# Moving shares and the Q projection in the attention schedule of a fused layernorm, attention and token-MLP kernel

## The chip, the cores and the metric

One core of one Trainium2 chip. The metric is the device time of one execution in microseconds, the median of several runs. The time before is 650.8 us (median of 3 runs, 650.64 to 651.08).

## What is computed

The output is the input, plus a segmented attention with a memory, plus an MLP over the token axis. Cut to what matters here (B = 1, S = 2048 tokens, D = 1024, 32 heads of 32, 4 segments of 512 tokens, F = 3584):

```python
x  = A_x; xn = layernorm(x)
q, k, v = heads(xn @ wq), heads(xn @ wk), heads(xn @ wv)      # 32 heads, 4 segments
for s in range(4):
    p     = softmax(q[s] @ k[s].T * scale + causal_mask)
    a_dot = p @ v[s]
    a_mem = phi(q[s]) @ M / (phi(q[s]) @ z + 1e-6)            # phi(t) = t+1 if t>0 else exp(t)
    o[s]  = g * a_mem + (1 - g) * a_dot
    M += phi(k[s]).T @ v[s];  z += phi(k[s]).sum(tokens)
A = o @ wo
B = (w2.T @ gelu(w1.T @ layernorm(xn) + b1) + b2)             # over the token axis
return x + A + B
```

## The kernel before

**Stages.** First the layernorm and the MLP, up to about 373 us of the profile, as dense products on TensorE; the MLP's result with the residual goes to the output tensor in DRAM as `part`. Then the attention, which is the only stage that the change touches.

**Units.** `attention` runs 32 units, one for each segment (8 units each) and group of four heads. Unit u does:

- *logits* of unit u in up to three steps, here written L(u,0), L(u,1), L(u,2). L(u,0) is key block 0, L(u,1) key blocks 1 and 3, and L(u,2), only in even units, is key block 2 of unit u and of unit u+1. Each step is 4 or 8 small matmuls into PSUM banks 0 to 3, one exponential on ScalarE over the four banks (line 1370), and one or two causal selects on POOL (line 1374).
- *weighing* of unit u-1 in three parts, W0, W1, W2: matmuls into bank 4, 5 and 4 again, each evicted by VectorE (line 1424). In segments 0 to 2, W2 also makes the update of the memory M, with two more VectorE operations (lines 1435, 1437).
- *dense jobs*, of 8 matmuls of 512 columns each: `v_job` (a chunk of V for later units, written here v m.c), `q_job(u + 2)`, `k_job(u + 2)` (up to unit 13), and `wo_job(c, half)` (an output projection of an earlier segment, written wo c.half). Dense jobs use banks 6 and 7 in turn. A job's first matmul waits until the job two before it has been read out of its bank. Who reads it out: ScalarE for q (line 1253) and for v from unit 8 on (line 1299); VectorE for k (save two), for earlier v, and for wo, an addition of `part` (line 1313).
- *side work* of VectorE, a queue `self.side`: `scales`, `products`, `add` (combining the weighed parts of unit u-1; lines 1467 to 1479), `phi_q(u)` (lines 1228, 1230), `phi_k`, and in twelve units one chunk of normalized x for a later segment ("xn": a VectorE scaling, line 1130, and a DMA transpose from SP's queue).

**What sets the order.** All of it is written out in program order, and each engine has its own in-order stream. `cut(total, shares)` turns a tuple of shares into numbers of dense matmuls: those ahead of L(u,0), then ahead of W0, of W1, of W2, of L(u,1), of L(u,2), and the rest. `dense(n)` issues n matmuls of the first jobs; when it has passed a *stop* (a count inside a job: 1, 3, 5, 7 on ScalarE's jobs and 1, 3, 5 on VectorE's in the later units), it issues one piece of side work behind the matmuls. When a job's eighth matmul has been issued, its read-out is issued at once.

A finished q (of unit 8 on) also needs its exponential `etmp` for phi; `late_exps` issues it behind the exponential of the next logits step:

```python
        fw.op("act", lambda e: e.activation(dst, src, ACT.Exp, scale=SCALE), ...)    # logits
        ...
        self.late_exps()                                                              # its last line

            if b is None:                                                             # dense
                b = job[1] = 6 + self.turn
                self.turn ^= 1
```

From unit 18 on, `unit_jobs` fills a quota (24 matmuls in even units, 20 in odd ones) with wo jobs. Where the quota ends inside a job, `self.left` carries its rest (4 matmuls) into the next unit. Before the change, the jobs of a unit stand in the order v, q, wo:

| unit | jobs in order (matmuls left of a carried one in brackets) | carried out |
|---|---|---|
| 18 | v5.2, q20, wo4.0 | |
| 19 | v5.3, q21, wo4.1 | 4 of wo4.1 |
| 20 | wo4.1 [4], v6.0, q22, wo5.0 | 4 of wo5.0 |
| 21 | wo5.0 [4], v6.1, q23 | |
| 22 to 25 | as 18 to 21, with v6.2 ... v7.1, q24 ... q27 | |
| 26, 27 | as 18, 19, with v7.2, v7.3, q28, q29 | 4 of wo7.1 |
| 28 | wo7.1 [4], q30, wo8.0, wo8.1 | 4 of wo8.1 |
| 29 | wo8.1 [4], q31, wo9.0 | |
| 30 | wo9.1, wo10.0, wo10.1 | |
| 31 | wo11.0, wo11.1 | |

In the units from 28 on, all waiting side work is issued ahead of W0. After unit 31 `tail` weighs unit 31 and makes the last four output projections.

Of the kernel before, what the change touches and what calls it, by code (L numbers as in the profile page):

```python
# [30 lines left out]
N_UNIT = N_SEG * N_GRP  # L31
# [355 lines left out]
class _Kernel:  # L387
# [1119 lines left out]
    def unit_jobs(self, u):  # L1507
        jobs = [self.wo_job(*self.wo_jobs.popleft())] if 10 <= u < self.QUOTA_FROM else []
        m = u // 4 + 1
        if m < 2 * N_SEG:  # L1510
            jobs.insert(0, self.v_job(m, u % 4))
        if u + 2 < N_UNIT:
            jobs.append(self.q_job(u + 2))
            if u + 2 < N_UNIT // 2:
                jobs.append(self.k_job(u + 2))
            else:
                self.k_load(u + 2)
        if u >= self.QUOTA_FROM:
            quota = self.QUOTA[u % 2] if u + 1 < N_UNIT else 100
            quota -= 8 * len(jobs) + sum(8 - j[0] for j in self.jobs)  # L1520
            while quota > 0 and self.wo_jobs:
                jobs.append(self.wo_job(*self.wo_jobs.popleft()))
                quota -= 8
            self.left = max(-quota, 0)
        return jobs
# [5 lines left out]
    def attention(self):  # L1531
        self.jobs, self.turn, self.left = deque(), 0, 0
        self.side, self.stops = deque(), self.STOPS
        self.exps, self.in_etmp = [], [None] * 4
        self.wo_jobs = deque((c, half) for c in range(4 * (N_SEG - 1)) for half in range(2))
        self.jobs.extend([self.q_job(0), self.k_job(0)] + [self.v_job(0, c) for c in range(4)])
        self.dense(16)
        self.late_exps()
        self.phi_k(0)
        self.k_transpose(0)  # L1540
        self.jobs.extend([self.q_job(1), self.k_job(1)])
        self.dense(100)
        for u in range(N_UNIT):
            if u == N_GRP:
                t, R = _Walk(self.mem, self.B_AT + self.STG_AT, self.B_AT + self.S2_AT).take(
                    "oT2", [P, N_GRP, SEG_L], BF16, N_GRP)
                self.oT.append(t)
                self.R_oT.append(R)
                self.load_fin(0)
                self.load_fin(1)  # L1550
            if 1 <= u <= N_GRP:
                self.fw.dma(self.wo[:, u - 1, :], self.A_wo[(u - 1) * P:u * P, :], writes=[self.R_wo[u - 1]])
            even = u % 2 == 0
            self.jobs.extend(self.unit_jobs(u))
            total = 8 * len(self.jobs) - sum(j[0] for j in self.jobs) - self.left
            xn = self.XN_AT.index(u) + 4 if u in self.XN_AT else None
            if u in self.XN_AT[::4]:
                self.xn_load(xn)
                self.xn_load(xn + 1)
            if u >= 18 and even:  # L1560
                cuts = self.cut(total, (0, 5, 1, 4, 0, 9, 5))
            elif u >= 18:
                cuts = self.cut(total, (4, 1, 2, 1, 0, 12))
            elif u < 10 or u >= 14 and total <= 26:
                cuts = self.cut(total, (0, 4, 2, 4, 1, 13, 8) if even else (7, 3, 2, 4, 1, 15))
            else:
                cuts = self.cut(total, (0, 4, 2, 2, 2, 14, 8) if even else (7, 3, 2, 2, 2, 16))
            end = u >= N_UNIT - 4
            self.stops = self.STOPS_FEW if total <= 26 and u >= 14 else self.STOPS
            self.dense(cuts[0])  # L1570
            self.logits(u, 0)
            self.dense(cuts[1], end)
            while end and self.side:
                self.side.popleft()()
            if u:
                self.weigh(u - 1, 0)
            self.dense(cuts[2], False)
            if u:
                self.weigh(u - 1, 1)
            self.dense(cuts[3], False)  # L1580
            if u:
                self.weigh(u - 1, 2)
                steps = self.combine(u - 1)
                last = steps[-1]
                steps[-1] = lambda u=u, last=last: (last(), self.o_transpose_dma(u - 1))
                self.side.append(steps.pop(0))
            if N_GRP <= u:
                self.side.append(lambda u=u: self.phi_q(u))
            if u:
                self.side.extend(steps)  # L1590
            if u + 1 < N_UNIT:
                self.side.append(lambda u=u: (self.phi_k(u + 1), self.k_transpose(u + 1)))
            if xn is not None:
                self.side.append(lambda c=xn: (self.xn_scale(c), self.xn_transpose(c), c % 4 < 2 and self.xn_load(c + 2)))
            self.dense(cuts[4])
            self.logits(u, 1)
            if even:
                self.dense(cuts[5])
                self.logits(u, 2)
            self.dense(8 * len(self.jobs) - sum(j[0] for j in self.jobs) - self.left)  # L1600
        while self.side:
            self.side.popleft()()
        self.tail()
# [84 lines left out]
```

## Time and profile before

| | |
|---|---|
| median of 3 runs | 650.8 us |
| profiled execution, time | 650.74 us |
| profiled execution, span from first to last instruction | 649.0 us |
| TensorE (PE) matmul busy | 644.7 us, 99% |
| VectorE (DVE) busy | 435.4 us, 67% |
| ScalarE (ACT) busy | 282.8 us, 44% |
| GpSimd (POOL) busy | 153.9 us, 24% |
| first L(0,0) to first L(31,1) | 387.44 to 628.68 us |

Times inside the profile are from the span's start. Matmul ends are modelled, and a matmul of 512 columns is shown as 380 ns long though the next one starts 216 ns later; so a busy PE may still be waiting, and waits are read from the starts: from the start of one step to the start of the next, less what the step takes elsewhere. ScalarE's and VectorE's shares are means over the whole span; in the attention ScalarE is busy 70 to 90% of the time.

### The profile page before, as it was taken

The numbers are of one execution on the slowest core, as the hardware profiler recorded it, in microseconds if no ns is written. First come the engines' busy times: TensorE is split into PE (matmuls) and PEld (weight loads), VectorE is DVE, ScalarE is ACT, GpSimd is POOL, SyncE is SP. The second block draws the span as 40 slices with busy tenths as digits, with TensorE's granted clock in tenths as the row PEclk, the third lists the DMA queues.
The fourth block names the chain that finished last, engine by engine and source line by source line (L and its number), as shares of the span: only waits on it lengthen the run. The fifth ranks groups of instructions, "written<-read, shape, count | busy, mean of one in ns | idle before, by whom it ended". The sixth has DMA issues, their size and how long they took to land.

```text
span 649.0 us, 11186 instructions
## 1 busy us (share of the span) xinstructions
PE 644.7 (99%) x4611; PEld 304.2 (47%) x4611; DVE 435.4 (67%) x813; ACT 282.8 (44%) x307; POOL 153.9 (24%) x179
## 2 busy tenths in 40 slices
PE   9999999999999999999999999999999999999998
PEld 3444444444444444444444444444455455545544
DVE  6975676665556664744647325766887888887886
ACT  6543232232210000110101037778777878889860
POOL 2500000000001220220202203344334444554450
PEclk9999999999999999999999999999999999999999
DMA  9804233233489947538272947999854675445334
GB/s 303 217 0 131 66 100 96 65 108 87 125 249 205 239 123 211 143 116 227 68 224 84 270 120 179 177 175 225 140 136 102 160 166 122 126 105 130 100 97 139
DMA packets 190123, 95.00 MB, mean 146 GB/s; under 512 B 108664, under 2 KB 176248, under 8 KB 190072
## 3 DMA queue, kind: packets, MB, share of 16 engines
q1 hardware_dynamic: 189928, 94.25, 57.6%
q8 instruction: 36, 0.59, 0.4%
q14 instruction: 15, 0.12, 0.1%
q10 hardware_dynamic: 144, 0.03, 0.0%
HBM read 69.23 MB, written 11.53 MB: 124 GB/s over the span
## 4 chain that ended last, share of the span: by engine, by line
PE 96%; ACT 2%; DVE 1%; DMA 0%; POOL 0%; issue 0%; DVEq 0%
PE ps_all L199 96%; ACT pT L1370 2%; DVE ln_st L587 1%; DMA xin<-in_A_x_dram 0%; DVE h L627 0%; POOL ln_rs L611 0%; ACT qT L1253 0%; ACT vA L1299 0%; DVE ln_mv L590 0%; DVE ln_mv L609 0%; DVE fin L1634 0%; PE ps_all L205 0%; DVEq L70 0%
## 5 line engine op out<-in xcount | busy, mean ns | idle before, releaser
L1370 ACT ACTIVATE pT<-ps_all 128x2048 bf16<-128x2048 f32 x80 | 150.1, 1877 | 41.2 <-PE ps_all L199 41.0
L1374 POOL TENSOR_SCALAR_AFFINE_SELECT pT<-pT 128x512 bf16<-128x512 bf16 x128 | 105.3, 841 | 159.2 <-ACT pT L1370 159.2
L689 DVE TENSOR_TENSOR part<-ps_all,part 128x512 f32<-128x512 f32 x84 | 57.7, 690 | 108.5 <-PE ps_all L199 87.5
L1075 POOL TENSOR_TENSOR part<-part,stg 128x512 f32<-128x512 f32 x24 | 33.0, 1402 | 284.8 <-DVE part L689 284.8
L746 ACT ACTIVATE g<-part,b1c 128x512 f16<-128x512 f32 x36 | 26.0, 722 | 98.7 <-DVE part L689 98.7
L199 PE MATMUL ps_all<-wv,xnT 128*128 128x512 bf16 x256 | 68.7, 380 | 0.3 <-ACT qT L1253 0.2
L199 PE MATMUL ps_all<-xnT,wq 128*128 128x512 bf16 x256 | 65.3, 380 | 0.0
L199 PE MATMUL ps_all<-wo,oT 128*128 128x512 bf16 (+2 forms) x272 | 63.6, 367 | 0.0
L694 ACT ACTIVATE part<-ps_all 128x512 f32<-128x512 f32 x24 | 14.0, 597 | 101.8 <-PE ps_all L199 67.1
L199 PEld LDWEIGHTS ps_all<-vA,pT 128*128 128x128 bf16 x1280 | 46.0, 96 | 17.2 <-DVE ost L1424 0.4
L1424 DVE TENSOR_TENSOR ost<-ps_all,eps 128x396 bf16<-128x396 f32 (+1 forms) x72 | 37.0, 522 | 24.6 <-PE ps_all L199 23.6
L199 PE MATMUL ps_all<-g,w2s 128*128 128x512 f16 x224 | 51.0, 379 | 0.0
L199 PE MATMUL ps_all<-g,sum 128*128 128x512 f16 x224 | 51.0, 379 | 0.0
L199 PE MATMUL ps_all<-gT,sum 128*128 128x512 f16 x224 | 50.3, 379 | 0.0
L199 PE MATMUL ps_all<-vA,pT 128*128 128x33 bf16 x1280 | 48.4, 177 | 0.0
L199 PE MATMUL ps_all<-h,sum 128*128 128x512 f16 x192 | 45.2, 379 | 0.0
L199 PE MATMUL ps_all<-h,w1s 128*128 128x512 f16 x192 | 44.9, 379 | 0.0
L199 PE MATMUL ps_all<-hT,sum 128*128 128x512 f16 x192 | 43.6, 379 | 0.0
L1473 DVE TENSOR_TENSOR prod<-ost,srec 128x1024 bf16<-128x1024 bf16 (+1 forms) x31 | 36.2, 1166 | 0.3
L199 PEld LDWEIGHTS ps_all<-wo,oT 128*128 128x128 bf16 x272 | 23.9, 98 | 24.6 <-issue 3.9
L199 PEld LDWEIGHTS ps_all<-xnT,wq 128*128 128x128 bf16 x256 | 22.7, 97 | 26.9 <-issue 5.3
L199 PEld LDWEIGHTS ps_all<-g,w2s 128*128 128x128 bf16 x224 | 21.9, 98 | 26.4
(119 smaller groups left out, 863.9 us busy)
## 6 DMA issues: line engine op xcount, KB each, us to landing
w2s<-in_B_w_dram SPq DMA_DIRECT2D x8, 1792.0 KB, 9.8
w1s<-in_B_w_dram SPq DMA_DIRECT2D x12, 1024.0 KB, 5.6
wq<-in_A_wq_dram SPq DMA_DIRECT2D x32, 256.0 KB, 3.3
xs<-in_A_x_dram SPq DMA_DIRECT2D x24, 256.0 KB, 3.2
stg<-in_A_x_dram SPq DMA_DIRECT2D x16, 256.0 KB, 2.9
out_dram<-stg SPq DMA_DIRECT2D x16, 256.0 KB, 3.7
wk<-in_A_wk_dram SPq DMA_DIRECT2D x16, 256.0 KB, 3.5
fin<-out_dram SPq DMA_DIRECT2D x16, 256.0 KB, 3.1
```

The source lines that it names most:

```text
L199: ins = self.nc.tensor.matmul(*args, **kwargs)
L587: fw.op("dve", lambda e: e.bn_stats(st[:, 6 * h:6 * h + 6], src[:, 512 * h:512 * h + 512]), reads=[self.R_xin[c]], writes=[R])
L689: self.fw.op("dve", lambda e: e.tensor_tensor(self.tmp[dst][:], self.bank(b), self.tmp[src][:], op=ALU.add), reads=[self.R_bank[b], self.R ...
L694: self.fw.op("act", lambda e: e.activation(self.tmp[dst][:], self.bank(b), ACT.Copy), reads=[self.R_bank[b]], writes=[self.R_tmp[dst]])
L746: self.fw.op("act", lambda e: e.activation(self.gB[f % 2][half][:, f // 2, :], src, ACT.Gelu_apprx_tanh, bias=self.b1c[:, f:f + 1], scale= ...
L1075: fw.op("pool", lambda e: e.tensor_tensor(self.tmp[t][:], self.tmp[t][:], self.stg[k][:, 512 * half:512 * half + 512], op=ALU.add), reads= ...
L1370: fw.op("act", lambda e: e.activation(dst, src, ACT.Exp, scale=SCALE), reads=self.R_bank[0:4], writes=[R[v % 2][kb] for v, kb, _ in blocks ...
L1374: fw.op("pool", lambda e: e.affine_select(d, d, pattern=[[0, 4], [1, P]], compare_op=ALU.is_ge, fill=0.0, base=0, channel_multiplier=-1), ...
L1424: fw.op("dve", lambda e: e.tensor_tensor(dst, src, eps, op=ALU.add), reads=[self.R_bank[b], self.R_eps], writes=[self.R_ost[o][part]])
L1473: fw.op("dve", lambda e: e.tensor_tensor(self.prod[:, a0:a1], ost[:, a0:a1, 0:D_HEAD], rec[:, a0:a1].unsqueeze(2).to_broadcast([P, a1 - a0 ...
```

## The change

Three edits, in `unit_jobs` and in the shares of `attention`.

```diff
@@ unit_jobs
             while quota > 0 and self.wo_jobs:
-                jobs.append(self.wo_job(*self.wo_jobs.popleft()))
+                jobs.insert(-1 if u + 2 < N_UNIT else len(jobs), self.wo_job(*self.wo_jobs.popleft()))
                 quota -= 8
@@ attention
             if u >= 18 and even:
                 cuts = self.cut(total, (0, 5, 1, 4, 0, 9, 5))
-            elif u >= 18:
+            elif 10 < u < N_UNIT - 1 and not even:
                 cuts = self.cut(total, (4, 1, 2, 1, 0, 12))
+            elif u == 0:
+                cuts = self.cut(total, (0, 4, 2, 4, 0, 9, 5))
             elif u < 10 or u >= 14 and total <= 26:
                 cuts = self.cut(total, (0, 4, 2, 4, 1, 13, 8) if even else (7, 3, 2, 4, 1, 15))
```

- *Order of jobs, units 18 to 29.* The wo jobs go ahead of the last entry, which is the q job: v, wo, q. The carried half job is then q21 into unit 20, q22 into 21, q25 into 24, q26 into 25, q29 into 28 and q30 into 29.
- *Odd units 11, 13, 15, 17* get the shares of the odd units from 18 on: in units 11 and 13 the cuts become 6, 2, 3, 2, 0, 19 (from 7, 3, 2, 2, 2, 16), in 15 and 17 they become 5, 1, 2, 2, 0, 14 (from 5, 3, 1, 3, 1, 11). L(u,1) follows W2 with no dense matmul between.
- *Unit 0:* cuts 0, 4, 2, 4, 0, 9, 5 (from 0, 3, 1, 4, 0, 10, 6). *Unit 31:* cuts 4, 1, 1, 2, 0, 8 (from 3, 1, 2, 0, 0, 10).

No instruction is added or removed; the number of matmuls, activations, VectorE operations and DMAs is the same.

## Prediction

> **What bounds the kernel now.** I read the page's busy shares and chain of waits first, then TensorE's own waits, then the timelines of the units that the change touches.
>
> ```profile
> PE 644.7 (99%) x4611; PEld 304.2 (47%) x4611; DVE 435.4 (67%) x813; ACT 282.8 (44%) x307; POOL 153.9 (24%) x179
> PE 96%; ACT 2%; DVE 1%; DMA 0%; POOL 0%; issue 0%; DVEq 0%
> PE ps_all L199 <- ACT pT L1370: 0.3, 2, 0.2
> PE ps_all L199 <- ACT qT L1253: 0.2, 1, 0.2
> ```
>
> The bound is TensorE's stream: 96% of the chain is matmuls, so a wait taken out or put in moves the end one for one. There is little to take out. The chain enters ScalarE at 387.9, 549.9, 579.4 and 624.4 us, and only there. I read the waits from starts on TensorE's timeline: eight dense matmuls are 1.73 us (0.216 each), a logits step 0.33, and going from a full-array matmul to logits costs about 0.10 everywhere (80 steps, in any order, so no edit removes it). What exceeds these from the first L to the tail is 0.23 ahead of L(0,1), 0.25 at v6.1 in unit 21, 0.16 at v7.1 in unit 25, 0.21 ahead of L(31,0), 0.06 in W2 of unit 31, 0.08 in W2 of unit 16. **A perfect change gains 1.0 us, 0.15%.** Here is unit 20 on TensorE (start, length, operation), then on ScalarE:
>
> ```profile
> 549.42 0.40 PE L199 MATMUL ps_all<-qT,kT 32*128 32x384 bf16 x8
> 549.75 0.60 PE L199 MATMUL ps_all<-wv,xnT 128*128 128x512 bf16 x2
> 550.19 1.67 PE L199 MATMUL ps_all<-xnT,wq 128*128 128x512 bf16 x7
> 551.80 0.40 PE L199 MATMUL ps_all<-qT,kT 32*128 32x256 bf16 x8
> 552.13 0.39 PE L199 MATMUL ps_all<-xnT,wq 128*128 128x512 bf16 x1
> 552.36 1.89 PE L199 MATMUL ps_all<-wo,oT 128*128 128x512 bf16 x8
> 554.76 0.38 PE L199 MATMUL ps_all<-wv,xnT 128*128 128x512 bf16 x1 [0.18 <-ACT qT L1253]
> ```
> ```profile
> 547.58 0.62 ACT L1219 ACTIVATE etmp<-qT 128x512 bf16<-128x512 bf16 x1
> 549.87 1.88 ACT L1370 ACTIVATE pT<-ps_all 128x2048 bf16<-128x2048 f32 x1 [1.67 <-PE ps_all L199]
> 551.64 0.59 ACT L1299 ACTIVATE vA<-ps_all 128x512 bf16<-128x512 f32 x1
> 552.25 1.88 ACT L1370 ACTIVATE pT<-ps_all 128x2048 bf16<-128x2048 f32 x1
> 554.02 0.59 ACT L1253 ACTIVATE qT<-ps_all 128x512 bf16<-128x512 f32 x1
> ```
>
> q22's last matmul stands behind L(20,2), so its copy stands behind that exponential and ends at 554.61; v6.1, which needs q22's bank, could start at 554.51 and starts at 554.76. From the rows: an exponential starts 0.45 after its L; a small ScalarE operation adds 0.50 to 0.60 to the queue; TensorE goes on 0.15 after the copy that frees a bank. VectorE in unit 19:
>
> ```profile
> 542.43 0.43 DVE L1424 TENSOR_TENSOR ost<-ps_all,eps 128x264 bf16<-128x264 f32 x1 [0.34 <-PE ps_all L199]
> 543.31 0.35 DVE L1467 RECIPROCAL srec<-ost 128x32 f32<-128x32 bf16 x1
> 544.12 0.69 DVE L1230 SCALAR_TENSOR_TENSOR pqT<-qT,mtmp 128x512 bf16<-128x512 bf16 x1
> 544.73 1.72 DVE L1473 TENSOR_TENSOR prod<-ost,srec 128x512 bf16<-128x512 bf16 x2
> 546.49 0.74 DVE L1479 TENSOR_TENSOR o_s<-prod 128x512 bf16<-128x512 bf16 x1
> 547.15 0.68 DVE L1313 TENSOR_TENSOR fin<-ps_all,fin 128x512 bf16<-128x512 f32 x1
> ```
>
> From L(19,1) at 542.33 VectorE has no gap until 548.8. A wo read-out issued here waits behind all of it.
>
> **What the Trainium skill says.** PSUM — Partial Sum Buffer (Engine vs sequencer instructions): "ScalarE/VectorE/GpSimdE queues are strict FIFO". The rows agree: vA and qT copies stand behind exponentials. My steps rest on this. TensorE: Matmul & The Clock Gate (Back-to-back issue gap) gives 216 ns for 512 columns; the trace's 1.73 us for eight agrees. SBUF — State Buffer (SBUF: two separate sides): a VectorE operation with two SBUF inputs and a GpSimd operation share a port pair as an exclusive lock, whoever starts first. The trace agrees in kind: `products` in one piece takes 1.22 us where POOL's select starts with it, 1.65 elsewhere.
>
> **The change, part by part.** Equal instructions throughout; only waits change.
>
> *Unit 0.* Ten dense matmuls instead of eight ahead of L(0,1): 387.44 + 0.33 + 2.16 + 0.10 = 390.03, past the exponential's end at 389.77. The wait goes: **-0.23**. L(0,2) then comes at 392.40, next to the exponential's end at 392.36: 0 (0 to +0.1).
>
> *Odd units 11 to 17.* L(u,1) comes 0.65 us earlier. L(15,0) to L(15,1) is still 0.33 + 5 x 0.216 + W 1.47 = 2.9 us against 2.38 for the exponential (0.45 + 1.88 + 0.05): no wait there now, none after. POOL's selects move with it, none is late. The stops shift, so the xn chunks of units 16 and 18 are issued in 15 and 17, with their VectorE scaling (0.54 to 0.85) and SP transpose. At unit 15's end VectorE then runs to about 517.6 instead of 517.5, and W2, which waited 0.08 for bank 4, waits about 0.1 more. In unit 16 wo3.0's addition falls behind `products`, as in unit 14, where v4.3 waited 0.06. **+0.15** (0 to 0.5).
>
> *q last, units 18 to 31.* SP: the wq load of q+2 is issued 1.7 us later, with most of two units (over 20 us) to land in 3.3; the output store and `fin` load go earlier; kT loads stay. Nothing waits. What moves is who frees which bank:
>
> - *v6.0 in unit 20, v7.0 in 24* now follow wo4.1 and wo6.0 in their bank, not a q. wo4.1's addition stands behind `phi_q` and `products`: it starts about 546.4 (1.65 after `products`), ends 547.06, releases at 547.12. TensorE reaches v6.0 at 546.55. Two waits of 0.57: **+1.14**. *wo8.0 in unit 28* follows wo7.1 in the same way, without memory update (0.5 less): `products` starts at 602.51, release at 604.91, reached at 604.74: **+0.17**.
> - *q22 in unit 20, q26 in 24* follow v6.0 and v7.0. q21 now finishes behind L(20,0), so its etmp comes behind L(20,1): exponential, etmp, vA copy. From L(20,1): 0.45 + 1.77 + 0.55 + 0.59 + 0.15 = 3.5. TensorE is there at 552.36 - 549.42 = 2.94. Two waits of 0.55: **+1.10** (0.9 to 1.3). The exponential of L(20,2) is pushed by 0.5 as well, which that wait covers.
> - *v6.1 and v7.1* now follow a wo whose addition ends about 5.06 after L(20,1); TensorE is there at 5.62. The old waits go: **-0.41**.
> - *wo9.0 in unit 29* follows wo8.1. In unit 28 VectorE now has two additions: wo8.0's goes in ahead of `scales`, from 608.34, and pushes `scales`, `phi_q`, `products`, `add` by 1.0. wo8.1's addition ends at 612.95; with `products` at 1.65 instead of 1.22, at 613.4. TensorE is there at 612.47: **+0.75** (0.5 to 1.0).
> - Where VectorE or ScalarE frees a bank elsewhere (v5.3, v6.3, v7.3, wo10.0) I find over 0.5 us of margin: 0.
>
> *Unit 31.* Four dense matmuls instead of three ahead of L(31,0) cover the 0.21; W2 no longer meets L(31,1) early: **-0.27**. wo11.0's addition now goes ahead of W2's eviction, and the tail's bank is free.
>
> Sum: -0.23 + 0.15 + 1.14 + 0.17 + 1.10 - 0.41 + 0.75 - 0.27 = **+2.4 us**. The profiled execution took 650.74 (span 649.0 and 1.74 around it), the median is 650.8, so the two agree: 650.8 + 2.4 = **653.2**. With every unknown at its lower end +1.8, at its upper +3.3.
>
> **The rivals.**
>
> *VectorE's additions are not late.* The point: from L(19,1) to v6.0 TensorE has 0.43 + 0.33 + 16 x 0.216 = 4.22 us. If the addition of wo4.1 is done within that (`products` fast, or the read-out getting ahead of it), the waits at v6.0, v7.0, wo8.0, wo9.0 fall away: 2.06 less, +0.3, **651.1**, not slower by what can be measured. For it: in units 16 and 17 before, additions stood ahead of `products`. Against: from unit 19 on the stops issue `products` at 5 matmuls and the read-out at 8.
>
> *More falls behind.* A stalled TensorE changes when POOL's selects meet VectorE; `products` at 1.65 instead of 1.22 in units 20 and 24 would make v6.1 and v7.1 wait, and late evictions hold W2. 0.3 us in each of four to five places: **654.5**. For it: VectorE is busy 80 to 90% in these slices. Against: each wait also gives it time.
>
> *Only the covers work.* If etmp doesn't stand ahead of the vA copy either, all that is left is the gain: **649.9**, no change by this measure. The program order speaks against it.
>
> **How the numbers follow.** About 0.2% (1.3 us, beyond 649.5 or 652.1) is what a measurement of this kernel can tell from no change. My sum 0.64, more falling behind 0.18, additions in time 0.13, only gains 0.05. The first two lie above 652.1, save a little of the first: slower 0.81, same 0.18, faster 0.01 (the gain is capped at 1.0). The likeliest is 653.2; the range leaves out the two low cases and the far end: 651.6 to 654.6.
>
> **What would show it.** Right: in unit 20 and 24 gaps of about 0.55 us at both v m.0 and q, the first released by L1313, the second by vA L1299; one at wo9.0 in unit 29; none at L(0,1), v6.1, v7.1, L(31,0). On ScalarE the order pT, etmp, vA, pT in units 20 and 24. Wrong: no gap at v6.0 (then VectorE was in time), or gaps in odd units 11 to 17 above 0.5.

## The result and the profile after

The changed kernel takes 652.61 us (median of 6 runs, 652.52 to 652.96) against 650.93 us (6 runs, 650.64 to 651.08) for the kernel before, on the same chip. The ratio is 1.0027, with a 95% interval of 1.0014 to 1.0040: slower by 1.7 us. The forecast was 653.2 us, slower, with a range of 651.6 to 654.6. The profiled execution's span is 651.0 us, against 649.0.

The stretch from the start of L(0,0) to the tail's first matmul takes 243.74 us before and 245.56 after, 1.82 more. The rest of the difference of the spans lies ahead of it: L(0,0) starts 0.24 later, and in the profiles of this document that start lies anywhere from 387.28 to 388.13, so the stretches are compared below and not the spans. The page of the changed kernel has the chain by engine, and TensorE's waits in the attention now name two engines (columns: total us, times, longest):

```profile
PE 93%; DVE 3%; issue 2%; DMA 1%; ACT 1%; DVEq 0%
```
```profile
PE ps_all L199 <- ACT vA L1299: 1.5, 4, 0.6
PE ps_all L199 <- DVE fin L1313: 1.2, 4, 0.5
```

Before, the chain was 96% TensorE, and its waits here were on `pT` and `qT`, 0.5 us in all. Now they are on V's copies and on the read-outs of wo. (In this trace 52 of 4611 matmul records are missing, so that some rows count one matmul too few, and part of what stands under vA is a missing record. The waits below are read from the starts of the rows around them; q_last_alone further down has the same six waits with no record missing.) Unit 20 on TensorE:

```profile
545.66 1.04 PE L199 MATMUL ps_all<-xnT,wq 128*128 128x512 bf16 x4
547.17 0.38 PE L199 MATMUL ps_all<-wv,xnT 128*128 128x512 bf16 x1 [0.48 <-DVE fin L1313]
...
550.04 0.40 PE L199 MATMUL ps_all<-qT,kT 32*128 32x384 bf16 x8
...
552.75 0.39 PE L199 MATMUL ps_all<-wo,oT 128*128 128x512 bf16 x1
553.73 1.67 PE L199 MATMUL ps_all<-xnT,wq 128*128 128x512 bf16 x7 [0.59 <-ACT vA L1299]
555.34 0.39 PE L199 MATMUL ps_all<-qT,kT 32*128 32x512 bf16 x4
555.66 0.39 PE L199 MATMUL ps_all<-wv,xnT 128*128 128x512 bf16 x1
```

Four matmuls of q21 from 545.66 end their issue at 546.52; v6.0 starts at 547.17, 0.65 us late. q22 could start at 552.97. Its row has seven of its eight matmuls; counted back one matmul, it began at 553.52, 0.55 us late. v6.1 follows L(21,0) after 0.32 us: its old wait is gone. VectorE in unit 19 and ScalarE in unit 20 show what was waited for:

```profile
544.10 0.69 DVE L1230 SCALAR_TENSOR_TENSOR pqT<-qT,mtmp 128x512 bf16<-128x512 bf16 x1
544.71 1.72 DVE L1473 TENSOR_TENSOR prod<-ost,srec 128x512 bf16<-128x512 bf16 x2
546.35 0.68 DVE L1313 TENSOR_TENSOR fin<-ps_all,fin 128x512 bf16<-128x512 f32 x1
```
```profile
550.49 1.88 ACT L1370 ACTIVATE pT<-ps_all 128x2048 bf16<-128x2048 f32 x1 [2.34 <-PE ps_all L199]
552.26 0.62 ACT L1219 ACTIVATE etmp<-qT 128x512 bf16<-128x512 bf16 x1
552.78 0.59 ACT L1299 ACTIVATE vA<-ps_all 128x512 bf16<-128x512 f32 x1
553.25 1.88 ACT L1370 ACTIVATE pT<-ps_all 128x2048 bf16<-128x2048 f32 x1
```

wo4.1's last matmul was issued by 544.4, but its read-out stands behind `products` and ends at 547.03; v6.0 begins 0.14 later. The copy of v6.0 ends at 553.37, with etmp between the exponential and it; q22 begins 0.15 later. ScalarE had stood idle for 2.34 us just ahead of this.

All waits read from the starts in the stretch, in us (beyond what a step takes elsewhere and the 0.10 for going to logits):

| place | before | after |
|---|---|---|
| ahead of L(0,1) | 0.23 | 0 |
| v4.3, v5.1 | 0.05, 0 | 0.05, 0.05 |
| W2 of unit 16 | 0.08 | 0 |
| v6.0, v7.0 | 0 | 0.65, 0.57 |
| q22, q26 | 0 | 0.55, 0.55 |
| v6.1, v7.1 | 0.25, 0.16 | 0 |
| wo8.0, wo9.0 | 0 | 0.25, 0.22 |
| ahead of L(31,0), W2 of unit 31 | 0.21, 0.06 | 0 |
| sum | 1.04 | 2.89 |

The difference, 1.85, is the stretch's 1.82 within the 0.01 to which each wait can be read.

### The profile page after: what moved, and what is told of

It is laid out like the page before. It is cut to its first block, busy times and chain, and to the rows that moved or that the text cites. A ratio compares the mean times of both kernels' runs of the same rounds, so it can differ in the third digit from the quotient of the medians.

```text
span 651.0 us, 11123 instructions
## 1 busy us (share of the span) xinstructions
PE 639.7 (98%) x4559; PEld 304.2 (47%) x4611; DVE 434.0 (67%) x813; ACT 282.1 (43%) x307; POOL 149.1 (23%) x179
## 4 chain that ended last, share of the span: by engine, by line
PE 93%; DVE 3%; issue 2%; DMA 1%; ACT 1%; DVEq 0%
PE ps_all L199 93%; DMA w2s<-in_B_w_dram 1%; ACT pT L1370 1%; DVE fin L1313 1%; DVE sum L648 0%; DVE pqT L1230 0%; DVE prod L1473 0%; DVE ost L1424 0%; DVE part L689 0%; DVE srec L1467 0%; ACT etmp L1219 0%; ACT vA L1299 0%; DVE mtmp L1228 0%; DVE gT L663 0%; DVE srec L1468 0%
## 5 line engine op out<-in xcount | busy, mean ns | idle before, releaser
L1374 POOL TENSOR_SCALAR_AFFINE_SELECT pT<-pT 128x512 bf16<-128x512 bf16 x128 | 100.6, 803 | 165.9 <-ACT pT L1370 165.9
L199 PE MATMUL ps_all<-wv,xnT 128*128 128x512 bf16 x239 | 65.8, 380 | 2.1 <-DVE fin L1313 0.9
L199 PE MATMUL ps_all<-wo,oT 128*128 128x512 bf16 (+2 forms) x257 | 61.2, 366 | 2.0 <-issue 0.8
L199 PE MATMUL ps_all<-xnT,wq 128*128 128x512 bf16 x242 | 61.2, 379 | 1.9 <-ACT vA L1299 1.2
L199 PEld LDWEIGHTS ps_all<-gT,sum 128*128 128x128 f16 x224 | 21.8, 98 | 26.8 <-DVE gT L663 0.6
```

What stands on the lines that cost most here:

```text
L199: ins = self.nc.tensor.matmul(*args, **kwargs)
L1374: fw.op("pool", lambda e: e.affine_select(d, d, pattern=[[0, 4], [1, P]], compare_op=ALU.is_ge, fill=0.0, base=0, channel_multiplier=-1), ...
```

## The experiments

All were timed beside the kernel before, whose median was 650.7 to 650.8 us in these runs (650.93 where the changed kernel was timed). The ratio is to the kernel before. The stretch is that from L(0,0) to the tail in each one's profile.

| kernel | median us | ratio, 95% interval | stretch us |
|---|---|---|---|
| before | 650.7 to 650.8 | 1 | 243.74 |
| changed kernel | 652.61 | 1.0027, 1.0014 to 1.0040 | 245.56 |
| q_last_alone | 653.37 | 1.0040, 1.0026 to 1.0054 | 246.11 |
| ends_alone | 650.37 | 0.9993, 0.9984 to 1.0001 | 243.25 |
| odd_alone | 650.85 | 1.0000, 0.9992 to 1.0008 | 243.70 |
| early_etmp | 651.67 | 1.0013, 1.0007 to 1.0020 | 244.54 |
| readout_first | 650.81 | 1.0001, 0.9993 to 1.0010 | 243.86 |
| both_mended | 649.75 | 0.9986, 0.9980 to 0.9993 | 242.83 |
| add_ahead_28 | 652.79 | 1.0032, 1.0020 to 1.0044 | 245.92 |
| add_ahead_wo81 | 653.26 | 1.0037, 1.0025 to 1.0050 | 246.31 |
| ends_and_shift | 650.16 | 0.9992, 0.9984 to 1.0000 | 243.24 |
| ends_and_shift_both | 649.96 | 0.9987, 0.9980 to 0.9994 | 242.86 |

**The theory:** all that is lost comes from the order of the jobs, by two in-order queues that free the banks of dense jobs: VectorE's (wo's read-out behind `products`) and ScalarE's (etmp ahead of V's copy). **The rivals:** the new shares of the odd units carry part of the loss; or the late jobs wait for their operands' DMAs or other inputs rather than for a bank.

### One part alone: q_last_alone, ends_alone, odd_alone

q_last_alone is the kernel before with this edit only:

```diff
-                jobs.append(self.wo_job(*self.wo_jobs.popleft()))
+                jobs.insert(-1 if u + 2 < N_UNIT else len(jobs), self.wo_job(*self.wo_jobs.popleft()))
```

> The kernel before with the first edit alone: wo jobs ahead of the q job from unit 18 on; all shares as before. Theory (bank turns): the six new waits seen in the changed kernel come all from this edit (0.63 + 0.57 at v6.0 and v7.0, 0.55 + 0.55 at q22 and q26, 0.25 at wo8.0, 0.22 at wo9.0: 2.77 us), the two at v6.1 and v7.1 go (-0.41): 650.9 + 2.4 = 653.3. The waits ahead of L(0,1) and L(31,0) stay. Rival (the shares of the odd units 11 to 17, or a sum of small losses, carry part of it): under 652.6.

Measured: 653.37 us. Its trace has the six new waits (0.66, 0.55, 0.57, 0.55, 0.25, 0.22), those of 0.23 ahead of L(0,1) and 0.21 ahead of L(31,0) stay. The whole loss lies in this edit.

ends_alone:

```diff
-            elif u >= 18:
+            elif 18 <= u < N_UNIT - 1:
                 cuts = self.cut(total, (4, 1, 2, 1, 0, 12))
+            elif u == 0:
+                cuts = self.cut(total, (0, 4, 2, 4, 0, 9, 5))
```

> The kernel before with the shares of unit 0 and of unit 31 alone. Theory: the waits of 0.23 ahead of L(0,1), 0.21 ahead of L(31,0) and 0.06 in W2 of unit 31 go and nothing takes their place: 650.9 - 0.5 = 650.4. Rival (a later wait takes up what is gained ahead of it, in the tail above all): 650.8 to 650.9.

Measured: 650.37 us, the stretch 0.49 shorter. By the times alone the interval still touches 1; the profile shows both waits gone and nothing in their place.

odd_alone:

```diff
-            elif u >= 18:
+            elif u >= 18 or 10 < u and not even:
```

> The kernel before with the shares of units 11, 13, 15 and 17 alone. Theory: L(u,1) comes 0.65 us earlier in these units, where no logits step waits before or after: 650.9, within 0.1. Rival (the earlier logits relieve ScalarE later, or the shifted side work makes W2 of unit 16 wait): 650.6, or 651.2 and more.

Measured: 650.85 us, the stretch 0.04 shorter, no difference by the times. In its trace W2 of unit 16 has lost its 0.08, and v5.1 has gained 0.05. The rival that the odd units carry part of the loss falls; nor do they gain.

### The two queues mended: early_etmp, readout_first, both_mended

early_etmp, on the changed kernel:

```diff
             self.dense(cuts[1], end)
+            if u in (20, 24):
+                self.late_exps()
```

> The changed kernel, but in units 20 and 24 the exponential of q21 and q25 (etmp) is issued right behind their copies, ahead of L(20,1) and L(24,1), where ScalarE is idle for 2.3 us. Theory (etmp ahead of the vA copy holds the bank that q22 and q26 need): the two waits of 0.55 go, 652.6 - 1.1 = 651.5; v6.1 and v7.1 then have under 0.1 us of margin and may wait that much. Rival (q22 and q26 wait for something else, such as their weights' DMA): 652.6.

Measured: 651.67 us, the stretch 1.02 shorter than the changed kernel's. ScalarE's timeline in unit 20 of this kernel:

```profile
548.00 0.59 ACT L1253 ACTIVATE qT<-ps_all 128x512 bf16<-128x512 f32 x1
548.62 0.63 ACT L1219 ACTIVATE etmp<-qT 128x512 bf16<-128x512 bf16 x1
550.94 1.88 ACT L1370 ACTIVATE pT<-ps_all 128x2048 bf16<-128x2048 f32 x1 [1.69 <-PE ps_all L199]
552.71 0.59 ACT L1299 ACTIVATE vA<-ps_all 128x512 bf16<-128x512 f32 x1
```

etmp now lies in the idle time, V's copy comes right behind the exponential, and q22 and q26 wait 0.03 each instead of 0.55 (v6.1 waits 0.03 too); the four waits on VectorE are as before. The edit leaves the loads of q22's and q26's weights alone, so it wasn't they that were waited for.

readout_first, on the changed kernel:

```diff
+            if u in (19, 23, 27, 28):
+                self.stops = (self.stops[0], (1, 3))
             self.dense(cuts[0])
```

> The changed kernel, but in units 19, 23, 27 and 28 a wo job takes side work at its matmuls 1 and 3 only, no longer at 5, so that VectorE gets its read-out (the addition to fin) ahead of products. Theory (the read-out behind products holds the bank): the waits at v6.0 0.63, v7.0 0.57, wo8.0 0.25 and wo9.0 0.22 go: 652.6 - 1.67 = 650.9. The waits at q22 and q26 stay. Rival (these jobs wait for their operands, or the delayed products makes the next W2 or a later read-out wait instead): 652 to 652.6.

Measured: 650.81 us. The four waits on wo's read-out are gone, those at q22 and q26 (0.55 each) are left. VectorE in unit 19 of this kernel:

```profile
543.83 0.69 DVE L1230 SCALAR_TENSOR_TENSOR pqT<-qT,mtmp 128x512 bf16<-128x512 bf16 x1
544.43 0.68 DVE L1313 TENSOR_TENSOR fin<-ps_all,fin 128x512 bf16<-128x512 f32 x1
545.04 1.72 DVE L1473 TENSOR_TENSOR prod<-ost,srec 128x512 bf16<-128x512 bf16 x2
```

These are the same operations in another order, and TensorE shows no wait for the later `products`.

both_mended has both edits.

> The changed kernel with both mends: etmp of q21 and q25 ahead of L(20,1) and L(24,1), and the wo read-outs of units 19, 23, 27 and 28 ahead of products. Theory: the two causes are separate and all six waits go, while the gains at L(0,1), v6.1, v7.1 and L(31,0) stay: 652.6 - 2.77 = 649.8, 1.0 below the kernel before. Rival (ScalarE's queue from L(20,1) to L(21,0) is longer than TensorE's work whatever the order, so that a wait comes back at v6.1 or L(21,0)): 650.3 to 650.8.

Measured: 649.75 us, ratio 0.9986: faster than the kernel before by 0.9 us (the interval excludes 1), and than the changed kernel by 2.9 (the stretch by 2.73). Of these waits 0.03 each at q22 and q26 is all that is left. TensorE in unit 20, from L(20,2) on:

```profile
551.66 0.40 PE L199 MATMUL ps_all<-qT,kT 32*128 32x256 bf16 x8
551.99 0.39 PE L199 MATMUL ps_all<-wo,oT 128*128 128x512 bf16 x1
552.24 1.89 PE L199 MATMUL ps_all<-xnT,wq 128*128 128x512 bf16 x8
554.06 0.40 PE L199 MATMUL ps_all<-qT,kT 32*128 32x512 bf16 x4
554.39 0.39 PE L199 MATMUL ps_all<-wv,xnT 128*128 128x512 bf16 x1
```

Every start follows the last by what its work takes, but for 0.03 ahead of q22 (0.25 from wo's matmul at 551.99, where 0.216 is the work). The rival that ScalarE's queue brings a wait back at v6.1 or L(21,0) falls.

### The term that was too large: add_ahead_28, add_ahead_wo81

The prediction gave wo9.0 a wait of 0.75 and the changed kernel has 0.22 (L(29,0) takes 0.33). TensorE at wo9.0, then VectorE in unit 28 of the changed kernel:

```profile
614.25 0.40 PE L199 MATMUL ps_all<-qT,kT 32*128 32x512 bf16 x4
614.80 0.39 PE L199 MATMUL ps_all<-wo,oT 128*128 128x512 bf16 x1 [0.15 <-DVE fin L1313]
```

```profile
612.49 1.65 DVE L1473 TENSOR_TENSOR prod<-ost,srec 128x1024 bf16<-128x1024 bf16 x1
614.07 0.68 DVE L1313 TENSOR_TENSOR fin<-ps_all,fin 128x512 bf16<-128x512 f32 x1
614.67 0.83 DVE L1479 TENSOR_TENSOR o_s<-prod 128x512 bf16<-128x512 bf16 x1
```

The read-out of wo8.1 stands ahead of `add`; the prediction had it behind. A first try to put it behind:

```diff
+            if u == 28:
+                self.stops = (self.stops[0], (1, 3, 5, 7))
             self.dense(cuts[0])
```

> The changed kernel, but in unit 28 a wo job also takes side work at its matmul 7, so that add goes to VectorE ahead of wo8.1's read-out, as the prediction had it. Theory (the term for wo9.0 was too large by just this operation, 0.66 us of VectorE): wo9.0 waits 0.22 + 0.66 = 0.88 us, 652.6 + 0.65 = 653.2. Rival (the wait at wo9.0 is ended by something else): 652.6.

Measured: 652.79 us, and wo9.0 waits 0.59, not 0.88. The edit did more than was meant: the stop at 7 also holds for wo8.0 and moved `scales` ahead of wo8.0's read-out, where VectorE was idle for 0.43 us in the changed kernel. VectorE in add_ahead_28:

```profile
609.67 0.35 DVE L1467 RECIPROCAL srec<-ost 128x32 f32<-128x32 bf16 x1
610.06 0.19 DVE L1468 TENSOR_TENSOR srec<-srec,gate 128x32 f32<-128x32 f32 x1
610.17 0.68 DVE L1313 TENSOR_TENSOR fin<-ps_all,fin 128x512 bf16<-128x512 f32 x1
```

So the second try gives that stop to wo8.1 alone, through the job's last field:

```diff
+            if u == 28:
+                self.stops = self.stops + ((1, 3, 5, 7),)
...
-        return [0, None, lambda: self.R_wo + self.R_oT[s % 3], mm, end, True]
+        return [0, None, lambda: self.R_wo + self.R_oT[s % 3], mm, end, 2 if (c, half) == (8, 1) else 1]
```

> The changed kernel, but wo8.1 in unit 28, and no other job, takes add as side work at its matmul 7, so that VectorE gets add ahead of wo8.1's read-out; the add_ahead_28 kernel also moved scales ahead of wo8.0's read-out, into time in which VectorE was idle. Theory (the prediction's term for wo9.0 was too large by add): add starts when products has ended (1.65 + 0.03 after its start), takes 0.66 of the queue, and the read-out comes 0.76 later: wo9.0 waits 0.98 instead of 0.22, 652.6 + 0.76 = 653.4. Rival (the wait at wo9.0 doesn't follow from add): 652.6 to 652.8.

Measured: 653.26 us. VectorE and then TensorE in this kernel:

```profile
612.51 1.66 DVE L1473 TENSOR_TENSOR prod<-ost,srec 128x1024 bf16<-128x1024 bf16 x1
614.20 0.74 DVE L1479 TENSOR_TENSOR o_s<-prod 128x512 bf16<-128x512 bf16 x1
614.86 0.68 DVE L1313 TENSOR_TENSOR fin<-ps_all,fin 128x512 bf16<-128x512 f32 x1
```
```profile
614.28 0.40 PE L199 MATMUL ps_all<-qT,kT 32*128 32x512 bf16 x4
615.59 0.39 PE L199 MATMUL ps_all<-wo,oT 128*128 128x512 bf16 x1 [0.92 <-DVE fin L1313]
```

L(29,0) takes 0.33, so wo9.0 waits 0.98: one operation of 0.7 us, put ahead of a read-out, moved the end by its full length.

### The waits of before without touching the order: ends_and_shift, ends_and_shift_both

Both are the kernel before with the shares of units 0 and 31, and in units 20 and 24 other shares.

```diff
+            if u in (20, 24):
+                cuts = self.cut(total, (0, 5, 1, 3, 0, 10, 5))      # ends_and_shift
+                cuts = self.cut(total, (0, 5, 1, 3, 0, 9, 6))       # ends_and_shift_both, in its place
```

> The kernel before with the shares of units 0 and 31, and in units 20 and 24 one dense matmul moved from ahead of W2 to behind L(20,1) and L(24,1) (shares 0, 5, 1, 3, 0, 10, 5); the order of jobs as before. Theory: ScalarE's unbroken stretch from L(20,1) to v6.1 is 0.25 us longer than TensorE's work there, one more matmul in it takes 0.22 of the wait at v6.1 and 0.16 at v7.1: 650.9 - 0.5 - 0.38 = 650.0. Rival (W2 then comes too early for bank 4, which VectorE reads out until shortly before): 650.4.

Measured: 650.16 us, the stretch as in ends_alone: nothing gained. It was neither reason given: W2 doesn't wait, and v6.1 waits its 0.25 still. TensorE in unit 20:

```profile
551.50 0.40 PE L199 MATMUL ps_all<-qT,kT 32*128 32x256 bf16 x8
...
553.89 0.40 PE L199 MATMUL ps_all<-qT,kT 32*128 32x512 bf16 x4
554.46 0.38 PE L199 MATMUL ps_all<-wv,xnT 128*128 128x512 bf16 x1 [0.18 <-ACT qT L1253]
```

From L(20,2) to v6.1 it is 2.96 us, as before. The race starts at L(20,2), which had not moved; I had counted from L(20,1).

> The kernel before with the shares of units 0 and 31, and in units 20 and 24 both L(u,1) and L(u,2) one dense matmul earlier (shares 0, 5, 1, 3, 0, 9, 6); in ends_and_shift L(u,2) stayed where it was. Theory (the wait at v6.1 is counted from L(20,2): exponential and q22's copy take 0.45 + 1.88 + 0.50 + 0.15 = 2.98, TensorE's work 2.71, so one more matmul of 0.22 behind L(20,2) fills it): the wait at v6.1 falls from 0.25 to about 0.03, that at v7.1 from 0.16 to 0: 650.9 - 0.5 - 0.38 = 650.0. Rival (as in ends_and_shift, the wait stays because L(20,2) itself is held until the exponential of L(20,1) has ended): 650.4.

Measured: 649.96 us, ratio 0.9987. Now L(20,2) comes one matmul earlier:

```profile
551.29 0.40 PE L199 MATMUL ps_all<-qT,kT 32*128 32x256 bf16 x8
...
553.88 0.40 PE L199 MATMUL ps_all<-qT,kT 32*128 32x512 bf16 x4
554.25 0.38 PE L199 MATMUL ps_all<-wv,xnT 128*128 128x512 bf16 x1
```

It is still 2.96 us to v6.1, with one more matmul of work inside: 0.04 of wait is left. Shares alone, with the old order, reach what both_mended reaches (stretches of 242.86 and 242.83); no run here shows a gain that needs the new order of jobs.

## Why the prediction was right, point by point

- **The bound** was right: each wait put in or taken out showed in the time. The gains were capped as said: of the 0.99 us of waits that it listed in the stretch before, none is left after.
- **Unit 0 and unit 31**, -0.23 and -0.27: gone as said; ends_alone shows them worth 0.49 together.
- **v6.0, v7.0**, 1.14 forecast: 1.22 measured (0.65 and 0.57). The read-out started at 546.35, forecast 546.4; the hand-over to TensorE took 0.14 once instead of 0.06. **wo8.0**, 0.17: 0.25. readout_first shows the cause.
- **q22, q26**, 1.10: 1.10. early_etmp shows the cause. **v6.1, v7.1**, -0.41: -0.41.
- **wo9.0**, 0.75: 0.22. The failed step is "pushes `scales`, `phi_q`, `products`, `add` by 1.0": `add` doesn't belong in that list. A wo job takes side work at its matmuls 1, 3 and 5 only, so it takes three pieces, and `add` goes with the next job. `products` did take 1.65, as the upper bound allowed. With `add` put there, 0.98 (add_ahead_wo81): the prediction's own upper bound of 1.0.
- **Odd units 11 to 17**, +0.15: -0.03. The addition of unit 16 fell behind `products` as said, and v5.1 waits 0.05 for it. The step that failed is "at unit 15's end VectorE then runs to about 517.6": it used 0.73 us for `add`, which took 0.42 in its new place. VectorE was free at 517.25, and W2 of unit 16 no longer waited its 0.08.
- **`products` at "1.22 us where POOL's select starts with it, 1.65 elsewhere"** was half right: before the change it also takes 1.22 with no select running (at 470.51). The longer time comes where a select is already running; the last section has the figures. So 1.65 in unit 28, given as an upper bound, had a reason: before the change the select started 0.39 after `products`; after it one had been running since 611.88 when `products` started at 612.49.

Forecast 2.4, in the stretch 1.8: 0.53 of the difference is wo9.0, 0.18 is unit 16, and wo8.0 and v6.0 go the other way by 0.16; what is left is rounding. Both wo9.0 (0.5 to 1.0) and the odd units (0 to 0.5) fell below their own ranges, so that the sum came out at the lower end given for all unknowns together (+1.8). It held because the large terms, v6.0, v7.0, q22 and q26, were right in their cause as well as their size. The rival in which VectorE's additions come in time was wrong in units 19, 23, 27 and 28; that more falls behind did not happen, but for the 0.05 at v5.1, which the sum had.

## What to carry to other kernels

In this kernel, whose TensorE hardly rests, all that the new order of independent jobs changed for TensorE was who frees the bank of the job two before, and what stands ahead of that on its in-order queue. List, for each bank, the engine that frees it and every operation issued between its last matmul and its read-out; operations that nobody waits for soon (here `products` and etmp) belong behind the read-out, or in a stretch in which that engine idles. Before sizing a wait, write out the issue order itself: two misses here, `add` in unit 28 and the start of the race at L(20,1), were misread orders, not wrong durations. The third, `add` in unit 15, was a duration: look also at what POOL runs when a VectorE operation with two inputs in SBUF starts.

## What the runs showed of the hardware

- `add` (line 1479, two bf16 inputs in SBUF) takes 0.41 to 0.43 us or 0.73 to 0.84, and the traces show with what it goes: POOL's causal select (line 1374). In the twelve profiles all 171 `add`s that start while a select has been running take the longer time, and all 117 others the shorter. `products` in one piece takes 1.45 to 1.66 in the 81 places where it starts so, and 1.21 to 1.23 in the 47 with no select near its start; in the other 76 a select starts within 0.09 us of it, and both times occur. In these 171 and 81 places the excess is the rest of the select's time, less 0.14 to 0.15 us. POOL in unit 19, before and then after the change:

```profile
544.73 2.22 POOL L1374 TENSOR_SCALAR_AFFINE_SELECT pT<-pT 128x512 bf16<-128x512 bf16 x2 [2.13 <-ACT pT L1370]
```
```profile
544.71 2.22 POOL L1374 TENSOR_SCALAR_AFFINE_SELECT pT<-pT 128x512 bf16<-128x512 bf16 x2 [2.14 <-ACT pT L1370]
```

Before, `add` starts at 546.49, 0.46 ahead of the end of the selects, and takes 0.74; after, it starts at 546.95, just behind their end, and takes 0.41. This agrees in kind with the exclusive port pair of which the prediction speaks, whoever starts first. No run was made to separate the two engines, so that the pair is the cause is not shown.
- In the waits read here TensorE's first matmul into a bank starts 0.15 us after the end of ScalarE's copy out of it, and 0.05 to 0.14 us after the end of VectorE's read-out.
